# Layer 1 of one 384-token block: each 384-column matmul issued as a 256-column and a 128-column matmul

## The chip, the cores and the metric

The kernel runs on one core of a Trainium2 chip. The metric is device time in microseconds (us) for one execution, the median of the runs of one kernel. A profile is one further execution with the hardware profiler on; it has its own time.

## The reference, cut to what matters

The reference is a random-feature attention followed by a two-layer network with an ELU between the layers:

```python
q_p, k_p = phi(q_s), phi(k_s)          # exp(x @ omega.T - |x|^2/2 - max) / sqrt(128)
kv = einsum('bhsm,bhsd->bhmd', k_p, v);  z = sum(k_p, axis=2)
attn = einsum('bhsm,bhmd->bhsd', q_p, kv) / (einsum('bhsm,bhm->bhs', q_p, z)[..., None] + 1e-6)
x = attn.transpose(0, 2, 1, 3).reshape(4608, 512)
h = x @ w_in                           # layer 1: 512 -> 2048
g = where(h > 0, h, exp(min(h, 0)) - 1)
out = g @ w_out                        # layer 2: 2048 -> 512
```

There are 8 batches of 8 heads, 576 tokens each, so 4608 tokens of 512 features; the network's inner width is 2048.

## The kernel before, in words

The network is computed in a form that keeps nearly full fp32 precision at the matmul rate of the shorter type fp32r: every operand is split into a high part and a low remainder, and a product is the sum of three matmuls, high by high, high by low and low by high.

The 4608 tokens are taken in eight blocks of 384 (blocks 0 to 7; "the eighth block" is number 7) and then in three wide blocks of 512 tokens, which use a scheme with seven products instead of eight (functions `wide1` and `wide2`). Blocks 0 to 2 go through the 16 slices of 128 inner features in two halves, blocks 3 to 7 in one go. A step is one block and one slice f:

- `layer1` (from L1007): for each of four chunks c of 128 input features, three matmuls add into one PSUM tile `ph` of 128 inner features by 384 tokens: weights `wh` by tokens `xh` (L1021), `wh` by `xl` (L1022), `wl` by `xh` (L1023). The weights (128 by 128) are the stationary operand, the tokens the moving one. That is 12 matmuls of 384 columns a step. Each matmul carries its own weight load: the profile has one LDWEIGHTS for each MATMUL, also where two in a row have the same stationary operand.
- the ELU on that tile: ScalarE (L1030, L1031), then VectorE (L1034), then the split into two tiles `g` (L408, L1042).
- `layer2` (from L1046): for three groups of 128 tokens, three products in two halves of 256 columns each, added into the banks `acc` (L1057). That is 18 matmuls of 256 columns a step.

While block 7 runs, VectorE, ScalarE and the DMA queues also prepare the weights of the wide blocks (tiles `rw` and `tw`); the attention is over by then.

The order on each engine is made by a planner in the program: every piece of work is entered with an engine, an estimated cost and a due time (class `Plan`), and the planner writes out one fixed order for each engine. The cost that it is given for three matmuls of layer 1 is `mm(n, 3)` on L1027, and the change does not touch it. At run time the engines keep that order and wait for each other by semaphores.

The code around the change:

Of the kernel before, what the change touches and what calls it, by code (L numbers as in the profile page):

```python
# [25 lines left out]
NC = DM // P  # L26
# [115 lines left out]
class Plan:  # L142
# [19 lines left out]
    def op(self, eng, ns, due, fn, reads=(), writes=(), nbytes=0, alt=None, port=False, tiled=False):  # L162
        n = len(self.tasks)
        engs = {eng: (ns, 0.0)}
        for e, *t in alt or ():
            engs[e] = tuple(t)
        for e in engs:
            if e not in ("PE", "SP"):
                engs[e] = (engs[e][0] * SLACK, engs[e][1])
        f = fn if alt is not None else lambda e: fn()  # L170
        deps, bufs = set(), set()
        for k in reads:
            if k in self.writer:
                deps.add(self.writer[k])
            self.readers.setdefault(k, []).append(n)
        for k in writes:
            if k in self.writer:
                deps.add(self.writer[k])
            deps.update(self.readers.pop(k, ()))
            self.writer[k] = n  # L180
        for k in (*reads, *writes):
            b = k[0] if isinstance(k, tuple) else k
            if isinstance(b, Buf):
                bufs.add(b)
        deps.discard(n)
        for b in bufs:
            b.left += 1
        for b in bufs:
            if b.left == 1:
                b.need = sum(c.key == b.key and c.left == 1 for c in bufs)  # L190
        locks = [e for e in engs if e == "POOL" or e == "DVE" and port]
        self.tasks.append((engs, due, f, deps, bufs, nbytes, locks, tiled))
# [134 lines left out]
def other(kind, *engs):  # L327
    return () if ALT[kind] is None else [(eng, ns, ALT[kind]) for eng, ns in zip(engs[::2], engs[1::2])]


def mm(n, m=1):

    return m * ((227.2 if n == 512 else 0.467 * n) - (0 if n == 512 else 4 if n == 384 else 6.2))


def act(n, psum=False, ptr=False):
    return (55 if psum else 101) + 0.833 * n + (93 if ptr else 0)


def dve(n, fast=False):  # L340
    return 69 + n / (1.92 if fast else 0.96)
# [7 lines left out]
def performer_elu_kernel(  # L349
# [14 lines left out]
    nc = tc.nc  # L364
# [33 lines left out]
    xh = const.tile([P, NC, RING], F32R, name="xh")  # L398
    xl = const.tile([P, NC, RING], F32R, name="xl")
# [4 lines left out]
    def copy(e, dst, src):  # L404
        if e == "ACT":
            nc.scalar.copy(dst, src)  # L406
        else:
            nc.vector.tensor_copy(dst, src)  # L408
# [588 lines left out]
    def ring(blk):  # L997

        o = (blk * TB) % RING
        keys = []  # L1000
        for b in range(2):
            for half, (s0, n) in enumerate(((0, 256), (256, S - 256))):
                if o < b * S + s0 + n and b * S + s0 < o + TB:
                    keys += [(b, hp, half, e) for hp in range(NHP) for e in range(4)]
        return keys

    def layer1(F, due):  # L1007
        blk, f = STEPS[F][:2]
        o = (SLOT[blk] if blk > 2 else blk) * TB
        w = w1c.pop(F)  # L1010
        p = Buf(ps, [P, 512], F32, "ph", f"ph_{F}", 2)
        e = Buf(sb, [P, TB], F32, "e", f"e_{F}", 2)
        n = BLOCKS[blk]
        g = gt[F] = [Buf(sb, [P, 512], F32R, "g", f"g_{F}_{z}", 6) for z in range(2)]

        def ph():
            return p()[:, 0:n]

        def mms(c):
            wh, wl = w()[:, 0, c * P:(c + 1) * P], w()[:, 1, c * P:(c + 1) * P]  # L1020
            nc.tensor.matmul(ph(), wh, xh[:, c, o:o + n], start=(c == 0), stop=False)  # L1021
            nc.tensor.matmul(ph(), wh, xl[:, c, o:o + n], start=False, stop=False)  # L1022
            nc.tensor.matmul(ph(), wl, xh[:, c, o:o + n], start=False, stop=(c == NC - 1))  # L1023

        for c in range(NC):
            reads = [("x3h", SLOT[blk], c), ("x3l", SLOT[blk], c)] if blk > 2 else [(z, k) for k in ring(blk) if k[1] == c for z in ("xh", "xl")]
            op("PE", mm(n, 3), due + 0.5 * c, lambda c=c: mms(c), [*reads, (w, "h"), (w, "l")], (p, ("f", blk, f)) if c == 0 else (p, ("fl", blk, f)) if c == 3 else (p,))  # L1027
        due += 2

        op("ACT", act(n, True), due, lambda: nc.scalar.activation(e()[:, 0:n], ph(), AF.Relu, scale=-1.0), (p,), (e,))  # L1030
        op("ACT", act(n), due + 0.2, lambda: nc.scalar.activation(e()[:, 0:n], e()[:, 0:n], AF.Exp, scale=-1.0), (e,), (e,))  # L1031
        op(
            "DVE", dve(n), due + 0.8,
            lambda: nc.vector.scalar_tensor_tensor(ph(), e()[:, 0:n], -1.0, ph(), ALU.add, ALU.max), (p, e), (p,),  # L1034
        )
        first, second = ("ACT", act(n, True)), ("DVE", dve(n))
        if blk:
            first, second = second, first
        op(*first, due + 1.2, lambda x: copy(x, g[0]()[:, 0:n], ph()), (p,), (g[0],), alt=other("g_hi", *second))
        op(  # L1040
            "DVE", dve(n), due + 1.5,
            lambda: nc.vector.tensor_tensor(g[1]()[:, 0:n], ph(), g[0]()[:, 0:n].bitcast(F32), ALU.subtract),  # L1042
            (p, g[0]), (g[1],),
        )
# [606 lines left out]
    for n in range(len(SEGMENTS)):  # L1651
        blk, f0, f1 = SEGMENTS[n]
# [14 lines left out]
    for s in range(NSB):  # L1667
        n = NS0 + s
# [88 lines left out]
```

## Time and profile before

| | us |
|---|---|
| median of 2 runs | 999.24 |
| the runs | 998.59 and 999.88 |
| profiled execution | 997.4 |
| its span, first to last instruction | 995.6 |
| TensorE busy in the span | 980.9 (99%) |
| VectorE busy | 868.0 (87%) |
| ScalarE busy | 719.1 (72%) |

A matmul's busy time in the profile overlaps that of the next one, since matmuls are pipelined; so the cost of a matmul in a stream is read from the distance between the starts of two that follow each other, not from its own length. The same holds for weight loads. PE is the matmul side of TensorE, PEld its weight loads.

### The profile page before, as it was taken

The numbers are of one execution on the slowest core, as the hardware profiler recorded it, in microseconds if no ns is written. First come the engines' busy times: TensorE is split into PE (matmuls) and PEld (weight loads), VectorE is DVE, ScalarE is ACT, GpSimd is POOL, SyncE is SP. The second block draws the span as 40 slices with busy tenths as digits, with TensorE's granted clock in tenths as the row PEclk, the third lists the DMA queues.
The fourth block names the chain that finished last, engine by engine and source line by source line (L and its number), as shares of the span: only waits on it lengthen the run. The fifth ranks groups of instructions, "written<-read, shape, count | busy, mean of one in ns | idle before, by whom it ended". The sixth has DMA issues, their size and how long they took to land.

```text
span 995.6 us, 27205 instructions
## 1 busy us (share of the span) xinstructions
PE 980.9 (99%) x9282; PEld 942.8 (95%) x9282; DVE 868.0 (87%) x3205; ACT 719.1 (72%) x1985; POOL 517.0 (52%) x695
## 2 busy tenths in 40 slices
PE   9999999999999999999999999999999999999997
PEld 8788899999999999999999999999999999999997
DVE  6998887888789999998999998899999979878866
ACT  7877876787667877887788787745546777777774
POOL 2465666687467787887787876710002232222321
PEclk9999999999999999999999999999999999999999
DMA  7455777777776867676676767388978776766762
GB/s 240 143 195 165 251 258 270 246 246 234 246 232 218 260 198 240 214 246 206 227 234 217 232 218 234 118 282 284 333 257 311 264 233 207 235 219 201 231 189 64
DMA packets 94249, 226.40 MB, mean 227 GB/s; under 512 B 23072, under 2 KB 34976, under 8 KB 94112
## 3 DMA queue, kind: packets, MB, share of 16 engines
q1 hardware_dynamic: 94112, 224.67, 69.2%
q8 instruction: 74, 1.21, 0.5%
q14 instruction: 63, 0.52, 0.2%
HBM read 187.40 MB, written 37.22 MB: 226 GB/s over the span
## 4 chain that ended last, share of the span: by engine, by line
PE 81%; DVE 11%; ACT 3%; issue 2%; DMA 1%; POOL 1%; SPq 1%; DVEq 0%; POOLq 0%
PE acc L1057 22%; PE ph L1021 8%; PE acs L1567 8%; PE ph L1023 8%; PE ph L1022 8%; PE A L1409 5%; PE B L1409 4%; PE pn L878 3%; PE pkv L654 3%; PE ppq L586 3%; PE ppk L586 2%; PE ppq L520 1%; PE pkv L714 1%; DVE rw L411 1%; PE ppk L520 1%
## 5 line engine op out<-in xcount | busy, mean ns | idle before, releaser
L1057 PE MATMUL acc<-w2h,g 128*128 128x256 f32 x1536 | 273.8, 278 | 0.0
L1057 PEld LDWEIGHTS acc<-w2h,g 128*128 128x128 f32 x1536 | 225.6, 188 | 3.6 <-issue 3.5
L1021 PE MATMUL ph<-xh,w1c 128*128 128x384 f32 x512 | 175.7, 343 | 1.5 <-DVE g L1042 1.5
L1023 PE MATMUL ph<-xh,w1c 128*128 128x384 f32 x512 | 172.6, 337 | 0.0
L1022 PE MATMUL ph<-xl,w1c 128*128 128x384 f32 x512 | 172.4, 337 | 0.0
L411 POOL TENSOR_TENSOR gq<-yh,gq 128x256 fp32r<-128x256 f32 x48 | 41.9, 873 | 241.7 <-ACT gq L406 224.8
L1057 PE MATMUL acc<-w2l,g 128*128 128x256 f32 x768 | 150.6, 277 | 0.0
L1057 PEld LDWEIGHTS acc<-w2l,g 128*128 128x128 f32 x768 | 116.3, 188 | 0.0
L1030 ACT ACTIVATE e<-ph 128x384 f32<-128x384 f32 x128 | 62.5, 489 | 63.9 <-PE ph L1023 63.1
L1021 PEld LDWEIGHTS ph<-xh,w1c 128*128 128x128 f32 x512 | 96.1, 188 | 8.0 <-issue 3.7
L1023 PEld LDWEIGHTS ph<-xh,w1c 128*128 128x128 f32 x512 | 96.2, 188 | 0.0
L1022 PEld LDWEIGHTS ph<-xl,w1c 128*128 128x128 f32 x512 | 96.2, 188 | 0.0
L411 POOL TENSOR_TENSOR hq<-hq,den 128x512 f32<-128x512 f32 (+1 forms) x96 | 81.0, 849 | 27.2 <-DVE den L785 22.6
L411 POOL TENSOR_TENSOR tk<-xk,tk 64x576 fp32r<-64x576 f32 x48 | 68.8, 1433 | 45.3 <-ACT tk L406 20.2
L1034 DVE SCALAR_TENSOR_TENSOR ph<-e,ph 128x384 f32<-128x384 f32 x128 | 71.2, 556 | 15.7 <-ACT e L1031 14.9
L776 DVE CUSTOM_DVE_ANT_0 junk<-hq,pz 128x128 f32<-128x128 f32 (+1 forms) x320 | 74.3, 280 | 6.7 <-PE pz L754 5.3
L496 ACT ACTIVATE hk<-hk,nbk 128x128 f32<-128x128 f32 x216 | 68.5, 392 | 13.8 <-POOL nbk L612 13.3
L411 POOL TENSOR_TENSOR tq<-xq,tq 64x576 fp32r<-64x576 f32 x48 | 68.6, 1428 | 15.9 <-DVE tq L408 11.4
L1042 DVE TENSOR_TENSOR g<-ph,g 128x384 fp32r<-128x384 f32 x128 | 70.3, 550 | 7.0 <-ACT g L406 4.6
L496 ACT ACTIVATE hq<-hq,nbq 128x128 f32<-128x128 f32 x216 | 68.4, 396 | 3.8 <-POOL nbq L612 3.6
L1031 ACT ACTIVATE e<-e 128x384 f32<-128x384 f32 x128 | 67.5, 528 | 1.8
L968 POOL TENSOR_TENSOR u_w<-u_w,raw_w 128x512 int32<-128x512 int32 x32 | 43.1, 1350 | 45.2 <-DVE u_w L965 18.0
(208 smaller groups left out, 2644.5 us busy)
## 6 DMA issues: line engine op xcount, KB each, us to landing
w1c<-w1s SPq DMA_DIRECT2D x112, 512.0 KB, 4.3
wp<-w1t SPq DMA_DIRECT2D x48, 512.0 KB, 4.0
raw_w<-in_w_dram SPq DMA_DIRECT2D x32, 512.0 KB, 4.5
xk<-in_kx_dram SPq DMA_DIRECT2D x24, 576.0 KB, 5.6
xq<-in_qx_dram SPq DMA_DIRECT2D x24, 576.0 KB, 4.3
wp<-w1s SPq DMA_DIRECT2D x24, 512.0 KB, 4.7
v<-in_v_dram SPq DMA_DIRECT2D x32, 325.0 KB, 4.0
w1s<-w1c SPq DMA_DIRECT2D x16, 512.0 KB, 3.8
```

Of the source, the lines that this page charges most:

```text
L411: (nc.vector if e == "DVE" else nc.gpsimd).tensor_tensor(*args)
L496: nc.scalar.activation(h()[:, j, :], src(j), AF.Exp, bias=nb()[:, j:j + 1], scale=-1.0)
L776: nc.vector.tensor_tensor_reduce(out=junk()[r], in0=h()[r, j, :], in1=pz()[r, a * P:(a + 1) * P], scale=1.0, scalar=EPS, op0=ALU.mult, op1 ...
L1021: nc.tensor.matmul(ph(), wh, xh[:, c, o:o + n], start=(c == 0), stop=False)
L1022: nc.tensor.matmul(ph(), wh, xl[:, c, o:o + n], start=False, stop=False)
L1023: nc.tensor.matmul(ph(), wl, xh[:, c, o:o + n], start=False, stop=(c == NC - 1))
L1031: op("ACT", act(n), due + 0.2, lambda: nc.scalar.activation(e()[:, 0:n], e()[:, 0:n], AF.Exp, scale=-1.0), (e,), (e,))
L1034: lambda: nc.vector.scalar_tensor_tensor(ph(), e()[:, 0:n], -1.0, ph(), ALU.add, ALU.max), (p, e), (p,),
L1042: lambda: nc.vector.tensor_tensor(g[1]()[:, 0:n], ph(), g[0]()[:, 0:n].bitcast(F32), ALU.subtract),
L1057: nc.tensor.matmul(a()[:, c], x()[:, ts], w[:, f, c], start=(f == f0 and n == 0 and not c.start), stop=(f == f1 - 1 and n == 2 and c.start ...
L1409: nc.tensor.matmul(o, at(a, i), u[b][:, i], start=(start and fresh_bank and i == 0 and n == 0), stop=(i == 1 and n == 2), skip_group_check ...
L1567: nc.tensor.matmul(bank()[:, z * TH:(z + 1) * TH], g()[:, a * TH + z * P:a * TH + z * P + P], w(b), start=(j == 0 and z == 0 and m == 0), ...
```

## The change

In block 7 alone, each of the three products of a chunk is issued as two matmuls with the same stationary operand: one over the first 256 tokens of the block and one over the last 128. Both halves lie in the one PSUM bank of `ph`. The flag that begins an accumulation stands on the first matmul of the tile, the flag that ends it on the last. The other seven blocks go through the same new loop with a single piece of 384.

```diff
         def mms(c):
             wh, wl = w()[:, 0, c * P:(c + 1) * P], w()[:, 1, c * P:(c + 1) * P]
-            nc.tensor.matmul(ph(), wh, xh[:, c, o:o + n], start=(c == 0), stop=False)
-            nc.tensor.matmul(ph(), wh, xl[:, c, o:o + n], start=False, stop=False)
-            nc.tensor.matmul(ph(), wl, xh[:, c, o:o + n], start=False, stop=(c == NC - 1))
+            cut = ((0, 256), (256, n)) if blk == 7 else ((0, n),)
+            for k, (a, x) in enumerate(((wh, xh), (wh, xl), (wl, xh))):
+                for s0, s1 in cut:
+                    nc.tensor.matmul(
+                        p()[:, s0:s1], a, x[:, c, o + s0:o + s1],
+                        start=(c == 0 and k == 0 and s0 == 0), stop=(c == NC - 1 and k == 2 and s1 == n),
+                    )
```

The order on TensorE where block 7 begins, before (`ph` is the layer 1 tile, `acc` a layer 2 bank, `w1c` the layer 1 weights):

```order
L1057 MATMUL acc_0_1_10861<-w2h,g_1_11965 128x256 x2
L1021 MATMUL ph_12041<-xh,w1c_11930 128x384
L1022 MATMUL ph_12041<-xl,w1c_11930 128x384
L1023 MATMUL ph_12041<-xh,w1c_11930 128x384
L1057 MATMUL acc_0_2_10885<-w2h,g_0_11955 128x256 x2
```

and in the changed kernel, at the same place:

```order
L1061 MATMUL acc_0_1_10861<-w2h,g_1_11965 128x256 x2
L1024 MATMUL ph_12041<-xh,w1c_11930 128x256
L1024 MATMUL ph_12041<-xh,w1c_11930 128x128
L1024 MATMUL ph_12041<-xl,w1c_11930 128x256
L1024 MATMUL ph_12041<-xl,w1c_11930 128x128
L1024 MATMUL ph_12041<-xh,w1c_11930 128x256
L1024 MATMUL ph_12041<-xh,w1c_11930 128x128
L1061 MATMUL acc_0_2_10885<-w2h,g_0_11955 128x256 x2
```

Three matmuls have become six, and nothing else has moved: the work of layer 2 stands before and after them as it did. This repeats 64 times (16 steps of four chunks).

On VectorE the same instructions stand in the same order; only what they wait for differs. For the first step of block 7, before:

```order
L1034 SCALAR_TENSOR_TENSOR ph_12041<-e_12079,ph_12041 128x384 [waits Activation_49]
L411 TENSOR_TENSOR tw_12067<-tw_12067 128x256 [waits DVE_49]
L408 CAST g_0_12107<-ph_12041 128x384 [waits DVE_49,PE_49]
L411 TENSOR_TENSOR tw_12067<-tw_12067 128x256 [waits DVE_49]
L1042 TENSOR_TENSOR g_1_12116<-ph_12041,g_0_12107 128x384 [waits DVE_49,PE_49]
```

and in the changed kernel:

```order
L1038 SCALAR_TENSOR_TENSOR ph_12041<-e_12091,ph_12041 128x384 [waits PE_49,Activation_49]
L411 TENSOR_TENSOR tw_12079<-tw_12079 128x256 [waits DVE_49]
L408 CAST g_0_12125<-ph_12041 128x384 [waits DVE_49]
L411 TENSOR_TENSOR tw_12079<-tw_12079 128x256 [waits DVE_49]
L1046 TENSOR_TENSOR g_1_12137<-ph_12041,g_0_12125 128x384 [waits DVE_49]
```

The first instruction of the three that belong to layer 1 now names TensorE as well as ScalarE: it waits for the matmuls of its own tile, for which ScalarE, which it waits for anyway, has waited already.

## Rows read from the trace of the kernel before

**Rows 1.** Profile page: busy time of engines, granted clock, the chain's shares.

```profile
PE 980.9 (99%) x9282; PEld 942.8 (95%) x9282; DVE 868.0 (87%) x3205; ACT 719.1 (72%) x1985; POOL 517.0 (52%) x695
...
PEclk9999999999999999999999999999999999999999
...
PE 81%; DVE 11%; ACT 3%; issue 2%; DMA 1%; POOL 1%; SPq 1%; DVEq 0%; POOLq 0%
```

**Rows 2.** Stretches: block 7's layer 1, then the wide blocks in two parts.

```profile
core 0: us, PE busy (x) PEld busy (x) DVE busy (x) ACT busy (x) POOL busy (x), PEclk, DMA share, GB/s
682.22:746.04 63.82, 63.82 (x458) 63.82 (x457) 60.56 (x139) 31.05 (x65) 0.00 (x0) 1.00 0.88 300
746.04:830.00 83.96, 81.52 (x695) 79.94 (x695) 75.47 (x191) 62.13 (x173) 20.74 (x23) 1.00 0.76 258
830.00:995.60 165.60, 159.25 (x1390) 158.49 (x1388) 132.34 (x336) 117.38 (x324) 40.47 (x50) 0.99 0.61 193
```

**Rows 3.** L1021, 682 to 746 us: count, ns min/median/max, first and last start.

```profile
L1021 PEld LDWEIGHTS ph<-xh,w1c x64: 187/188/188, 682.1 to 745.3; 128*128 128x128 f32 x64
L1021 PE MATMUL ph<-xh,w1c x64: 332/334/336, 682.2 to 745.5; 128*128 128x384 f32 x64
```

**Rows 4.** Order of time inside block 7: start us, length us, engine, line.

```profile
692.84 0.33 PE L1021 MATMUL ph<-xh,w1c 128*128 128x384 f32 x1
692.84 0.19 PEld L1022 LDWEIGHTS ph<-xl,w1c 128*128 128x128 f32 x1
693.01 0.34 PE L1022 MATMUL ph<-xl,w1c 128*128 128x384 f32 x1
693.01 0.19 PEld L1023 LDWEIGHTS ph<-xh,w1c 128*128 128x128 f32 x1
...
693.18 0.34 PE L1023 MATMUL ph<-xh,w1c 128*128 128x384 f32 x1
693.19 0.19 PEld L1021 LDWEIGHTS ph<-xh,w1c 128*128 128x128 f32 x1
...
693.36 0.34 PE L1021 MATMUL ph<-xh,w1c 128*128 128x384 f32 x1
```

**Rows 5.** Chain, 746 to 790 us: twelve 256-column matmuls of the wide blocks.

```profile
788.69 1.36 PE acs L1567 x12
```

**Rows 6.** Lengths as in rows 3: L1409 from 746, L1021 from 50, L800.

```profile
L1409 PE MATMUL A<-xh,wp x96: 276/276/388, 748.1 to 823.9; 128*128 128x256 f32 x96
...
L1021 PE MATMUL ph<-xh,w1c x58: 332/336/448, 58.1 to 149.9; 128*128 128x384 f32 x58
...
L800 PEld LDWEIGHTS pt<-ident,hq x72: 137/140/197, 26.2 to 120.6; 128*128 128x128 f32 x72
L800 PE MATMUL pt<-ident,hq x72: 270/273/329, 26.3 to 120.7; 128*128 128x128 f32 x72
```

**Rows 7.** Order of time: PE at 768.8 us, where it had waited.

```profile
768.85 0.97 PE L1409 MATMUL A<-xh,wp 128*128 128x256 f32 x6 [0.25 <-DVE A L1364]
...
768.85 0.77 PEld L1409 LDWEIGHTS A<-xh,wp 128*128 128x128 f32 x6 [0.45 <-DVE A L1364]
```

**Rows 8.** Order of time in the attention: short matmuls, each with its load.

```profile
12.74 1.87 PEld L714 LDWEIGHTS pkv<-v,hk 128*128 128x128 f32 x16
12.85 1.90 PE L714 MATMUL pkv<-v,hk 128*128 128x65 f32 x16
...
26.23 0.90 PEld L800 LDWEIGHTS pt<-ident,hq 128*128 128x128 f32 x8
```

**Rows 9.** Waits of PE from 746 us on: total, times, longest.

```profile
PE A L1409 <- ACT c L406: 1.1, 1, 1.1
PE B L1409 <- DVE c L1433: 0.6, 1, 0.6
PE B L1409 <- DVE B L1364: 0.4, 2, 0.3
PE A L1409 <- DVE A L1364: 0.3, 1, 0.3
```

**Rows 10.** Order of time: end of block 7's last ELU on ScalarE and VectorE.

```profile
746.95 0.52 ACT L1031 ACTIVATE e<-e 128x384 f32<-128x384 f32 x1
...
747.92 0.56 DVE L1034 SCALAR_TENSOR_TENSOR ph<-e,ph 128x384 f32<-128x384 f32 x1
```

## The prediction

> **What bounds the kernel now.** I read the profile's page first: TensorE (PE) is busy for 99% of the span, its granted clock is at the higher of its two levels (2.4 GHz) in every slice, and the chain of work that ended last lies on PE for 81% [rows 1]. Then the stretches: block 7's layer 1 runs from 682.22 to 746.04 us, and PE is busy for 63.82 of these 63.82 us, with VectorE close behind at 60.56 [rows 2]. So inside the block nothing keeps PE waiting, and time that its instructions gain or lose there moves everything behind it, unless a later wait takes it up. After the block PE is idle for a little: 83.96 less 81.52 us up to 830 us [rows 2].
>
> A busy PE is not yet PE at its best, because matmuls overlap in the record. So the third view is the order of time, where I read only the starts. Three 384-column matmuls in a row start at 692.84, 693.01 and 693.18, and the next one at 693.36: 0.52 us for three, 0.173 each [rows 4]. For 256 columns the wide blocks give twelve in 1.36 us, 0.113 each [rows 5].
>
> The same view shows how weight loads hide. Each load starts at the same hundredth as the matmul in front of its own: 692.84 and 692.84, 693.01 and 693.01 [rows 4]. It runs one matmul ahead, never two. A load therefore has just one matmul's time in which to stay hidden, and the question is how long it really takes; its recorded 0.188 us [rows 3] is longer than a whole 256-column slot, so it overlaps the next load's and can't be the answer.
>
> Three rows give the answer. First, where PE had to wait and a matmul starts together with its own load, both at 768.85 [rows 7], the matmul is recorded with up to 388 ns where the usual one of its line has 276: 112 more. For layer 1 the same difference is 448 less 336, again 112 [rows 6]. That is a load with nothing to hide behind. Second, in the attention sixteen matmuls of only 65 columns, each with its own load, keep their loads (1.87 - 0.19) / 15 = 0.112 us apart [rows 8], though by the columns they should be quick. Third, the only matmuls with 128 moving columns that stand in an unbroken row, the transposes of L800, have loads (0.90 - 0.14) / 7 = 0.109 apart [rows 8]. A load of 128 weight columns in this type costs about 0.112 us. A 256-column matmul (0.113) just covers it, a 384-column one covers it easily, and a 128-column one cannot.
>
> **The change part by part.** It removes 64 x 3 = 192 matmuls of 384 columns (64 on each of three lines; [rows 3] has those of one) and puts in 192 of 256 and 192 of 128 columns, with 192 more loads. Nothing else is moved on PE.
>
> - Taken out: 64 runs of three at 0.52 us, 33.3 us.
> - The 256-column pieces: 192 x 0.113 = 21.7 us. During each of them the load for the 128-column piece runs, hidden.
> - The 128-column pieces: by columns they take 0.173 - 0.113 = 0.060 us (or half of 0.113, 0.057). In this time the load for the next 256-column matmul has to run, and it needs 0.112. The slot becomes 0.112, of which 0.052 is PE standing with the load uncovered. 192 x 0.112 = 21.5 us.
> - Sum: 21.7 + 21.5 - 33.3 = **+9.9 us** on PE. Every fourth triple ends a step and the next matmul is one of layer 2; its load is of the same kind and has the same 0.112 to run.
>
> The 128-column matmul in this type with its own load occurs nowhere before, so its slot has to be bounded. Below: if the load hid completely, 0.057, which makes the pair 0.170 instead of 0.173 and the change worth -0.6 us. Above: if the whole load stood bare ahead of each such piece, 0.057 + 0.112 = 0.169 [rows 6], +20.9 us. I take 0.112, because the rows nearest in shape (short moving side, a load each) lie at 0.109 and 0.112.
>
> The Trainium skill, "TensorE: Matmul & The Clock Gate", section "Back-to-back issue gap", speaks for the lower end: at full clock it puts the distance between matmuls at N / 2.4 + 2.5 ns, for which I estimate 56 for 128 columns, 109 for 256 and 162.5 for 384, so that the sum would be +0.5 us. The 65-column matmuls speak against its use here, since they go by their loads. The same section gives about 81 ns for 128 columns in a stream of loads and matmuls, by which the sum would be some +4 us.
>
> What else changes costs nothing. The wait for PE that the first VectorE instruction of each ELU now names is for matmuls that ScalarE has waited for before it. 192 more matmuls are 2% of 9282 [rows 1] and PE's queue shows no idle time in the block to which they could add.
>
> **What is given back.** A slower PE gives VectorE more time in a stretch where it was 95% busy. PE's idle time from 746 us on is 1.1 + 0.6 + 0.4 + 0.3 = 2.4 us, all of it on ScalarE and VectorE results [rows 9]; each such wait also bares a load. But VectorE can only use the gift as far as it was behind: at the end of the block its ELU instruction starts at 747.92, when its input was done at 746.95 + 0.52 = 747.47 [rows 10], so it lags by 0.45 us. I take 0.5 us given back; the bounds are 0 and 2.4 with some 0.11 for each of the five waits, 3.0.
>
> So the profiled execution goes from 997.4 to 997.4 + 9.9 - 0.5 = 1006.8 us. The median shown is 999.24, 1.8 above the profiled execution, so **1008.6 us** for the median.
>
> **The rivals.**
>
> *By columns (not slower).* If two matmuls in a row with the same stationary operand, or a load that can run further ahead, make the second load free, only columns count: 999.24 - 0.6 = 998.6 us, at best a touch faster than before. It decides as soon as the 128-column slot falls below 0.061 us. For it: nothing in the trace has exactly this shape, and the 65-column rows are of the slower fp32 kind, where one matmul makes two records. Against: layer 2 already issues pairs with the same stationary operand, with a load for each (9282 of both) [rows 1], and the loads in block 7 keep one matmul ahead [rows 4]. The skill's page of the paragraph above is the rule behind it. Chance 0.09; another 0.03 for a load half hidden, a slot near 0.084, 192 x 0.024 = +4.5 us, 1003.7 us.
>
> *All given back that can be.* The load bound holds, but VectorE and ScalarE reach the wide blocks with so much in hand that PE no longer waits for them: 999.24 + 9.9 - 3.0 = 1006.1 us. For it: the waits lie within 85 us of the block. Against: the lag is small, and the work that PE waits for is made from PE's own results. Chance 0.07.
>
> *The load bare at every second piece.* The upper bound: 999.24 + 20.9 = 1020.1 us, if a load did not start before the short matmul was done. Against: the 65-column matmuls, 0.112 with everything in it. Chance 0.03.
>
> **How the numbers follow.** The load-bound case with a small return has 0.78; its own range runs from slots of 0.109 (the transposes; 0.6 us less) to 0.115 (0.6 more), and from 0 to 1.5 us given back: 1007.0 to 1010.2 with some 0.5 for the runs' spread. The range that I give, 1004.5 to 1011, takes in the second rival as well and leaves out the 0.15 of the others. Two per cent, about what a measurement of this kernel can tell from no change, is 20 us: only the last rival passes it. Faster by over 2% has no case (0.01), slower by over 2% has 0.04, and 0.95 lies within.
>
> **What would show it.** Right: in block 7, starts of a 256- and a 128-column matmul 0.113 and about 0.112 us apart, loads too at that distance; the block some 10 us longer than 63.8, PE busy in all of it; VectorE's share in it down to about 82%; PE's waits after it at most as before. Wrong: 128-column starts followed within 0.06 us by the next, with a block of about 63 us; or a block ten us longer and an end that moved far less, which would make the waits the larger story; or a granted clock below its higher level inside the block, which no stretch here before 830 us shows [rows 2].

## The result and the profile after

The changed kernel takes 1010.57 us (median of 2 runs, 1009.92 to 1011.21) against 999.24 us, a ratio of 1.0113 with a 95% interval of 1.007 to 1.0157: some 11 us slower, where 9.4 were forecast. Five runs of it beside nine of before, below, give 1.0102 (1.0084 to 1.012). Its profiled execution takes 1011.21 us with a span of 1009.4.

The page answers to [rows 1]: 192 more matmuls and 192 more loads, the busy shares and the granted clock nearly as they were.

```profile
PE 993.1 (98%) x9474; PEld 954.2 (95%) x9474; DVE 869.2 (86%) x3205; ACT 719.3 (71%) x1985; POOL 515.7 (51%) x695
...
PEclk9999999999999999999999999999999999999999
...
PE 81%; DVE 10%; ACT 3%; issue 2%; DMA 2%; SPq 1%; POOL 0%; DVEq 0%; POOLq 0%
```

Cut into the same stretches as [rows 2], each moved to where block 7 and the wide blocks begin now (columns as there):

```profile
683.86:758.30 74.44, 74.44 (x650) 74.44 (x649) 62.48 (x141) 31.60 (x65) 0.00 (x0) 1.00 0.76 258
758.30:842.26 83.96, 80.88 (x683) 78.72 (x683) 73.66 (x184) 60.48 (x168) 19.16 (x22) 1.00 0.75 255
842.26:1009.40 167.14, 160.79 (x1403) 160.04 (x1402) 133.25 (x340) 118.84 (x328) 40.85 (x50) 0.99 0.60 193
```

Block 7 is 74.44 us long instead of 63.82, so 10.62 us of the difference lie in it, with PE busy throughout, VectorE's share down from 95% to 84% and the clock at its higher level. It begins 1.6 us later than before, which lies within the spread: two profiles of the kernel before (the second is below) begin it 4 us apart. And the stretch from its end to the last instruction is 251.1 us instead of 249.5, of which more below.

Inside the block the weight loads are the rows to read. This is the PEld side, in order of time (start, length, engine, line; neighbours of one line are merged, with their count):

```profile
701.93 0.30 PEld L1024 LDWEIGHTS ph<-xl,w1c 128*128 128x128 f32 x2
702.16 0.54 PEld L1024 LDWEIGHTS ph<-xh,w1c 128*128 128x128 f32 x4
702.63 0.30 PEld L1024 LDWEIGHTS ph<-xl,w1c 128*128 128x128 f32 x2
702.86 0.30 PEld L1024 LDWEIGHTS ph<-xh,w1c 128*128 128x128 f32 x2
703.09 0.30 PEld L1061 LDWEIGHTS acc<-w2h,g 128*128 128x128 f32 x2
```

Two loads, one pair of pieces, every 0.23 us: 702.63 to 702.86 to 703.09, and four from 702.16 to 702.63. Ten loads take 703.09 - 701.93 = 1.16 us, 0.116 each. Over the whole block, by the starts of the single loads, a short matmul's slot is 0.108 us on average and a long one's 0.122, 0.230 for the pair. A product now costs 0.23 us where a 384-column matmul took 0.173 [rows 4]. The forecast had 0.113 + 0.112 = 0.225.

The matmuls' own starts need care here. On this record a 256-column matmul starts about 0.06 us after the short one in front of it, and a short one some 0.17 us after the long one, as if the short matmul had been quick. I read this as a recorded start that lies ahead of the moment at which the weights are in: such a 256-column matmul is also recorded as longer, 0.334 us instead of 0.276 (rows below). Over a pair the two distances add to 0.23. The loads' starts show without this shift what paces the stream.

### The profile page after: what moved, and what is told of

Same layout as the page of the kernel before. It is cut to its first block, busy times and chain, and to the rows that moved or that the text cites. A ratio compares the mean times of both kernels' runs of the same rounds, so it can differ in the third digit from the quotient of the medians.

```text
span 1009.4 us, 27599 instructions
## 1 busy us (share of the span) xinstructions
PE 993.1 (98%) x9474; PEld 954.2 (95%) x9474; DVE 869.2 (86%) x3205; ACT 719.3 (71%) x1985; POOL 515.7 (51%) x695
## 4 chain that ended last, share of the span: by engine, by line
PE 81%; DVE 10%; ACT 3%; issue 2%; DMA 2%; SPq 1%; POOL 0%; DVEq 0%; POOLq 0%
PE ph L1024 24%; PE acc L1061 22%; PE acs L1571 8%; PE A L1413 5%; PE B L1413 4%; PE pn L878 3%; PE pkv L654 3%; PE ppq L586 3%; PE ppk L586 2%; PE ppq L520 1%; DMA xq<-in_qx_dram 1%; PE ppk L520 1%; PE pkv L714 1%; DVE rw L411 1%; DVE junk L776 1%
## 5 line engine op out<-in xcount | busy, mean ns | idle before, releaser
L1024 PE MATMUL ph<-xh,w1c 128*128 128x384 f32 (+2 forms) x1152 | 307.9, 325 | 1.5 <-DVE g L1046 1.5
L1024 PEld LDWEIGHTS ph<-xh,w1c 128*128 128x128 f32 x1152 | 201.5, 188 | 8.0 <-issue 3.7
L1024 PE MATMUL ph<-xl,w1c 128*128 128x384 f32 (+1 forms) x576 | 176.2, 324 | 0.0
L1024 PEld LDWEIGHTS ph<-xl,w1c 128*128 128x128 f32 x576 | 103.3, 188 | 0.0
L411 POOL TENSOR_TENSOR tq<-xq,tq 64x576 fp32r<-64x576 f32 x48 | 68.5, 1428 | 15.5 <-DVE tq L408 10.5
L408 DVE CAST g<-ph 128x384 fp32r<-128x384 f32 x112 | 61.4, 548 | 5.7 <-PE acc L1061 4.3
L600 DVE CUSTOM_DVE_ANT_0 hk<-ppk,p2k 128x128 f32<-128x128 f32 x216 | 52.5, 285 | 9.8 <-ACT p2k L406 8.4
```

What stands on the lines that cost most here:

```text
L411: (nc.vector if e == "DVE" else nc.gpsimd).tensor_tensor(*args)
L1024: nc.tensor.matmul(p()[:, s0:s1], a, x[:, c, o + s0:o + s1], start=(c == 0 and k == 0 and s0 == 0), stop=(c == NC - 1 and k == 2 and s1 == n),
```

## The experiments

Each kernel below is the changed one with one more edit, if nothing else is said. Times are medians, ratios against the kernel before on the same chip.

**The changed kernel again.**

> The changed kernel again, for the size of the difference. Load theory (a weight load costs some 0.11 us and can hide behind one matmul only): +9.4 us forecast on the median, +10.6 us by the length of block 7 in its first profile, so a ratio near 1.010. Rival, part of the first difference is spread of the executions outside the block: the block's length comes out at 74 us again, and what lies before and behind it changes by a us or two without order.

1009.48 us (5 runs) against 999.52 (9 runs): +10.0 us, ratio 1.0102 (1.0084 to 1.012). Its block 7:

```profile
684.43:758.87 74.44, 74.44 (x650) 74.44 (x649) 62.38 (x141) 31.60 (x65) 0.00 (x0) 1.00 0.76 257
```

To the hundredth the length of the first profile. So the block is the measure to compare kernels by: the timed difference has an interval of some 2 us to either side, the block's length none that can be seen.

**The cut at 192.**

```diff
-            cut = ((0, 256), (256, n)) if blk == 7 else ((0, n),)
+            cut = ((0, 192), (192, n)) if blk == 7 else ((0, n),)
```

> Block 7's layer 1 matmuls cut at 192 instead of 256: 192 + 192 columns. Load theory: 192 columns need about 0.087 us, less than a load, so both slots are load-bound, 0.108 to 0.112 each, a pair 0.216 to 0.224: +8.2 to +9.7 us against before. Columns theory (only columns count): no change. Fixed price for every extra matmul: as the 256 + 128 cut, +10.6 us.

1008.45 us, ratio 1.009 (1.0074 to 1.0105), +8.9 us. The block (the first row), and its loads in order of time:

```profile
681.22:755.09 73.87, 73.87 (x650) 73.87 (x649) 62.32 (x141) 31.57 (x65) 0.00 (x0) 1.00 0.77 260
```

```profile
700.86 0.31 PEld L1024 LDWEIGHTS ph<-xh,w1c 128*128 128x128 f32 x2
...
702.21 0.30 PEld L1061 LDWEIGHTS acc<-w2h,g 128*128 128x128 f32 x2
```

Twelve loads in 702.21 - 700.86 = 1.35 us, 0.1125 each, for 192 columns that would need some 0.087 us by the columns. Columns theory falls. The block is 10.05 us longer than before; a fixed price for every extra matmul would fit this run too.

**The cut at 320.**

```diff
-            cut = ((0, 256), (256, n)) if blk == 7 else ((0, n),)
+            cut = ((0, 320), (320, n)) if blk == 7 else ((0, n),)
```

> Cut at 320: 320 + 64 columns. Load theory: the 320-column slot is some 0.143 us by its columns, the 64-column slot still a whole load, 0.108 to 0.112, a pair 0.251 to 0.255: +15 to +16 us, dearer than the 256 + 128 cut with the same columns and the same number of matmuls. Fixed price for every extra matmul: +10.6 us, as that cut. Columns theory: no change.

1015.5 us, ratio 1.0155 (1.014 to 1.0171), +16.0 us. The block is 79.64 us long, 15.82 more than before:

```profile
685.57:765.21 79.64, 79.64 (x650) 79.64 (x649) 62.64 (x141) 31.45 (x65) 0.00 (x0) 1.00 0.71 241
```

The same columns and the same number of matmuls as in the change, and 5.2 us more in the block. A fixed price for every matmul falls here: the short slot doesn't get cheaper with its columns (0.108 us on average, as in the change), while the long one gets dearer (0.149). By the load, 64 columns leave more of it uncovered than 128.

**Three pieces of 128.**

```diff
-            cut = ((0, 256), (256, n)) if blk == 7 else ((0, n),)
+            cut = ((0, 128), (128, 256), (256, n)) if blk == 7 else ((0, n),)
```

> Three pieces of 128 columns: 384 extra matmuls and loads. Load theory: three slots of 0.108 to 0.112, 0.324 to 0.336 in place of 0.173: +29 to +31 us. Fixed price for every extra matmul, by the 256 + 128 cut: twice its cost, +21 us. Columns theory: no change.

1030.78 us, ratio 1.0312 (1.0295 to 1.0329), +31.3 us. Nine loads of short pieces, from 701.35 to 702.35:

```profile
701.35 0.75 PEld L1024 LDWEIGHTS ph<-xh,w1c 128*128 128x128 f32 x6
702.01 0.42 PEld L1024 LDWEIGHTS ph<-xl,w1c 128*128 128x128 f32 x3
702.35 0.75 PEld L1024 LDWEIGHTS ph<-xh,w1c 128*128 128x128 f32 x6
```

1.00 / 9 = 0.111 us for each 128-column matmul in an unbroken stream of them: the price of which the kernel before had no row, and nearly twice its 0.057 by the columns.

**256 + 256: columns for nothing.** The second piece is widened to 256 columns by taking the last 128 tokens twice; the second copy goes to bank columns that nothing reads.

```diff
+                    dst, src = p()[:, s0:s1], x[:, c, o + s0:o + s1]
+                    if s0:
+                        dst = p()[:, s0:512].rearrange("p (r x) -> p r x", r=2)
+                        src = src.unsqueeze(1).to_broadcast([P, 2, P])
```

> The 256 + 128 cut of block 7, but the second matmul has 256 columns: the last 128 tokens twice, the second time into 128 columns of the PSUM bank that nobody reads. 192 x 128 columns of added work. Load theory: a 256-column slot costs what a load costs, about 0.113, so a pair is 0.226 to 0.228: +10.1 to +10.5 us against before, the same as the 256 + 128 cut or less. Fixed price for every extra matmul, or columns theory: 192 x 0.056 = 10.7 us more than the 256 + 128 cut, +21 us against before.

1008.59 us, ratio 1.0079 (1.0057 to 1.0101), +8.1 us, and the block and its loads:

```profile
682.64:756.08 73.44, 73.44 (x651) 73.44 (x649) 62.20 (x141) 31.49 (x65) 0.00 (x0) 1.00 0.78 261
```

```profile
700.21 0.30 PEld L1028 LDWEIGHTS ph<-xh,w1c 128*128 128x128 f32 x2
...
701.57 0.30 PEld L1065 LDWEIGHTS acc<-w2h,g 128*128 128x128 f32 x2
```

This block does a third more columns in layer 1 than the changed kernel's and is 1.00 us shorter. Twelve loads take 701.57 - 700.21 = 1.36 us, 0.113 each. So 128 columns were free: the slot is as long without them. The block comes out lower than was expected, 9.6 us above before instead of 10.1 to 10.5. The layer 1 slots are the expected 0.113 each; what had not been thought of is layer 2, whose 264 slots in the block came down from 0.1154 us on average to 0.1133.

The timed kernels so far leave one rival that had not been written down: a least distance of some 0.11 us between any two matmuls, whatever sets it, would give all these times too. The traces speak against it. In the changed kernel PE waits before the matmul at 821.57 us, whose load starts together with it:

```profile
821.57 0.75 PEld L1413 LDWEIGHTS A<-xh,wp 128*128 128x128 f32 x6 [0.64 <-DVE A L1368]
821.57 0.95 PE L1413 MATMUL A<-xh,wp 128*128 128x256 f32 x6 [0.44 <-DVE A L1368]
822.36 0.84 PE L1571 MATMUL acs<-w_qh,gq 128*128 128x256 f32 x6
```

These six matmuls take 822.36 - 821.57 = 0.79 us, where six 256-column slots take 0.68. PE had just been idle, so a least distance had nothing to delay, and yet 0.11 us more are spent: the length of one load.

The recorded lengths say the same, though the profile models the ends of matmuls. The lines are from block 7 of the changed kernel (first two), the cut at 320 (next two), the cut at 192 (fifth) and the three pieces (last); the last number but one is the mean length in ns:

```profile
L1024 PE MATMUL ph<-xl,w1c 128*128 128x256 f32 x64 | 21.4, 334 | 0.0
L1024 PE MATMUL ph<-xl,w1c 128*128 128x128 f32 x64 | 14.3, 223 | 0.0
L1024 PE MATMUL ph<-xl,w1c 128*128 128x320 f32 x64 | 25.0, 391 | 0.0
L1024 PE MATMUL ph<-xl,w1c 128*128 128x64 f32 x64 | 12.3, 192 | 0.0
L1024 PE MATMUL ph<-xl,w1c 128*128 128x192 f32 x128 | 24.9, 276 | 0.0
L1024 PE MATMUL ph<-xl,w1c 128*128 128x128 f32 x192 | 31.9, 275 | 0.0
```

A 256-column matmul has 276 ns behind one of its kind, 334 behind one of 128 columns, and up to 388 with the whole load bare [rows 6]: 0, 58 and 112 more. A 128-column one has 223 behind a long one and 275 behind one of its kind, 52 more; a 320-column one 304 behind 256 columns and 391 behind 64, 87 more; a 192-column one 252 behind 256 columns and 276 behind one of its kind, 24 more. With 64, 128, 192 and 256 columns in front the wait falls from 87 to 0, as the part of a load does that they leave uncovered.

**The pieces grouped by length.** Within a chunk, three matmuls of 256 columns, then three of 128:

```diff
-            for k, (a, x) in enumerate(((wh, xh), (wh, xl), (wl, xh))):
-                for s0, s1 in cut:
+            for s0, s1 in cut:
+                for k, (a, x) in enumerate(((wh, xh), (wh, xl), (wl, xh))):
```

> The same 192 + 192 matmuls of 256 and 128 columns, in another order: within a chunk first the three of 256, then the three of 128. Load theory: still one load a matmul; the two 256-column matmuls that follow one of their kind go back to 0.113, the short ones are 0.108 to 0.112 as in the cut into three: a triple 3 x 0.113 + 3 x 0.110 = 0.669 or a little over, +9.5 us, about 1 us less than the alternating order (whose 256-column loads were 0.120 to 0.128 apart). Rival, the price belongs to the change of bank columns between pieces and not to the loads: a third of the changes are left (two of six against six of six), so +3 to +4 us.

1010.06 us, ratio 1.0093 (1.0077 to 1.011), +9.5 us; the block 74.26 us:

```profile
683.07:757.33 74.26, 74.26 (x650) 74.26 (x649) 62.37 (x141) 31.48 (x65) 0.00 (x0) 1.00 0.77 258
```

The rival that laid the price on changes of bank columns falls. But the block came down by 0.18 us and not by the 1 us that was expected. Over the 192 pairs, the few thousandths by which a mixed pair (0.229, 0.173 + 10.62 / 192) exceeds 0.113 + 0.111 are 0.9 us. The starts of the single loads show where they went: layer 1 did come down, from 44.18 to 43.50 us, but the 264 slots of layer 2 in the block went up from 30.31 to 30.82. So the alternation does cost something in layer 1, and the grouping moves most of it behind layer 1's short matmuls. What sets these thousandths stays open: only where all matmuls have 256 columns (256 + 256) is every slot in the block 0.113 to 0.114.

**The cut in block 5.**

```diff
-            cut = ((0, 256), (256, n)) if blk == 7 else ((0, n),)
+            cut = ((0, 256), (256, n)) if blk == 5 else ((0, n),)
```

> The 256 + 128 cut in block 5 instead of block 7, while the attention still runs beside it. Load theory with TensorE as the bound there too: the same 192 pairs, +10 us. Rival, TensorE has slack among the attention's waits in block 5 and takes the loads up: clearly less, +3 to +7 us.

1007.9 us, ratio 1.0079 (1.0063 to 1.0094), +7.4 us by the medians. Block 5 before, and then with the cut:

```profile
507.88:599.48 91.60, 91.59 (x985) 87.91 (x986) 86.19 (x425) 73.41 (x220) 72.73 (x112) 1.00 0.70 227
```

```profile
507.60:609.30 101.70, 101.66 (x1178) 98.41 (x1179) 87.15 (x427) 74.08 (x220) 73.59 (x112) 1.00 0.63 205
```

Block 5 is 10.1 us longer; in the ten other profiles, none of which cuts it, it is 91.1 to 92.5. TensorE is the bound there as well, attention or not, and the rival with slack falls by the block's length. The interval of the timed difference (6.3 to 9.4 us) lies a little below that, but the profile shows nothing given back behind the block: block 6 takes 82.7 us as before, block 7 63.82, and the rest 249.8. What the 2 to 3 us are stays open.

**Before, profiled once more.**

> The kernel before once more, for a second profile: block 7 again 63.8 us long; the time from its end to the last instruction shows whether the 1.2 to 2.2 us by which this stretch was longer in the profiles of the cut kernels is an effect of the cut (again 249.5 us here) or spread (250 to 252 us).

One run of 1002.33 us, with a span of 1000.5. Block 7 is again 63.82 us long:

```profile
686.31:750.13 63.82, 63.82 (x459) 63.82 (x458) 60.35 (x139) 30.94 (x65) 0.00 (x0) 1.00 0.87 300
```

It begins at 686.31 instead of 682.22, so one and the same kernel differs by 4 us ahead of the block. From the block's end to the last instruction it takes 1000.5 - 750.1 = 250.4 us. With the first profile, the block 5 kernel and the one below, four profiles without a cut in block 7 have 249.5 to 250.4 there, mean 249.9; seven with one have 250.3 to 251.7, mean 251.1. The two sets overlap, but in the profiles the cut kernels come out about 1 us longer behind the block, and none gets anything back. The timed runs don't show this 1 us: in the seven experiments with a cut block the timed difference lies from 2.7 us below to 0.4 above what that block gained in length, 0.9 below on average. So the time by the clock is less certain, by a us or two, than the length of the block.

**Longer matmuls instead of shorter ones.** The kernel before, with each pair of 256-column matmuls of layer 2 made into one of 512, in all eight blocks:

```diff
-                    for c in (slice(0, TH), slice(TH, DM)):
+                    for c in (slice(0, DM),):
```

> The kernel before with the opposite edit in layer 2 of all eight blocks: each pair of 256-column matmuls with the same stationary operand becomes one of 512 columns, 1152 in place of 2304, with half the loads. Load theory: a 256-column matmul just covers a load, so little is to be had: from 0 (two slots of 0.113 become 0.227) to -4 us (the slots of block 7's layer 2 were 0.1155 on average; if all of the 0.002 is the load's, 2304 x 0.002 = 4.6 us). Fixed price for every extra matmul of some 0.05 us: 1152 fewer would give some -60 us. Rival on the other side: long matmuls pay 0.451 ns a column, as the 384-column ones do, 0.231 a slot: 0 to +5 us.

1001.92 us (11 runs) against 1000.17 (15), ratio 1.0024 (1.0014 to 1.0035): slower by 1.8 us by the medians. In order of time on PE, three 512-column matmuls start at 702.00, 702.23 and 702.46, and the next matmul at 702.69:

```profile
702.00 0.39 PE L1057 MATMUL acc<-w2h,g 128*128 128x512 f32 x1
702.23 0.39 PE L1057 MATMUL acc<-w2l,g 128*128 128x512 f32 x1
702.46 0.39 PE L1057 MATMUL acc<-w2h,g 128*128 128x512 f32 x1
702.69 0.33 PE L1021 MATMUL ph<-xh,w1c 128*128 128x384 f32 x1
```

0.23 us each, 0.45 ns a column as with the 384-column ones; two 256-column ones had taken 0.227 [rows 5]. 1152 matmuls fewer gained nothing, so no fixed price shows for a matmul whose load is covered.

No kernel here beats the one before.

## Why the prediction was right, and where it was off

*The load costs 0.112 us and hides behind one matmul only.* Right, and shown in four ways: 0.111 and 0.1125 us a slot where every piece is short, a dearer pair when the short piece gets shorter (cut at 320), no dearer one when it gets columns for which the load's time is enough (256 + 256), and 0.11 us more where a load stands bare behind an idle PE. The rows of before that carried this were the pair of lengths with and without a covered load [rows 6, 7] and the loads of the 65-column matmuls [rows 8].

One row of the same group seemed to say otherwise and was passed over: the transposes of L800 have 329 ns at most and 273 as a rule [rows 6], which by the same subtraction makes a load of 56. The changed kernel explains it. A 128-column matmul with its load covered is recorded with 223 ns, so the usual 273 of a stream of them holds half a load already, and 329 - 223 = 106 is near the 109 that the forecast took from their loads.

Two readings of the prediction were wrong and cost it nothing: 32 of the 64 triples, not every fourth, have layer 2 behind them (the slot there is 0.108 us either way); and L520 and L654 have 128 moving columns in a row as well, though with a stationary operand of half the size.

*The sum on PE, +9.9 us.* Right in kind, 0.7 us too small: 10.62 by the block. The term that was mis-sized is the pair, put at 0.113 + 0.112 and measured at 0.230, and in it the long piece: 0.122 and 0.108. The sum had taken the 256-column slot from streams of that shape alone.

*The block stays bound by PE and the cost lies on the path.* Right: PE is busy for 74.44 of 74.44 us.

*0.5 us given back by VectorE.* Not borne out by the profiles, and with it the rival that gave back 3 us. The forecast took PE's waits behind the block for a backlog of VectorE's. The first three of them show that they are not. They come 19.1, 22.9 and 47.9 us after the block in the changed kernel, within 0.1 us of their places before. This is the largest, before and after, 19.07 and 19.14 us behind the block, and then the list of the changed kernel:

```profile
765.11 0.98 PE L1409 MATMUL A<-xl,wq 128*128 128x256 f32 x6 [1.10 <-ACT c L406]
777.44 0.98 PE L1413 MATMUL A<-xl,wq 128*128 128x256 f32 x6 [1.10 <-ACT c L406]
```


```profile
PE A L1413 <- ACT c L406: 1.1, 1, 1.1
PE A L1413 <- DVE A L1368: 0.7, 2, 0.4
PE B L1413 <- DVE B L1368: 0.7, 2, 0.5
PE B L1413 <- DVE c L1437: 0.5, 1, 0.5
```

That is nearly the list of [rows 9], which the 10 us that VectorE was given had no part in shortening. What sets them was not tried. What changed is a later place. The chain of waits of the kernel before leads there through the load of the next wide block's tokens (start, length, what):

```profile
800.00 6.36 DMA xw<-xd
806.38 0.62 ACT xl L406
```

and that of the changed kernel through the same load, 0.93 us longer:

```profile
812.19 7.29 DMA xw<-xd
819.51 0.62 ACT xl L406
```

Behind it PE waits for 0.44 us, at 821.57 us (the row above), at a place where it had not waited before. Both loads are issued some 54 us after the block's end (800.00 - 746.04 and 812.19 - 758.30). Why it lands later is not settled: in the four profiles without a cut in block 7 it has landed 59.7 to 60.7 us after the block, in the seven with one 60.7 to 61.7. Over the eleven profiles a later landing goes with a longer stretch from the block to the end (60.0 us with 249.8, 61.7 with 251.7), so the load is the likely source of the 1 us; no experiment tried it alone.

*The number.* The two misses, a pair 0.7 us too cheap and a return that did not come, point the same way and did not cancel. The first median, 1010.57 us, lies above the 1007.0 to 1010.2 that the prediction gave its main case, whose lower end also left out the 0.5 for the spread; the second, 1009.48, lies within. That the first fell within the wider range owes something to the margin.

*The rivals.* Columns alone: against the measured 0.111 us for 128 columns. The load bare at every second piece, +20.9 us: no, the block has half of that. The estimate of some +4 us from the figure of 81 ns in the Trainium skill, "TensorE: Matmul & The Clock Gate", section "Back-to-back issue gap", and that of +0.5 us from its N / 2.4 + 2.5, do not hold for these fp32r matmuls, each with its own load, where the slot is 111 ns. The section "LDWEIGHTS (loading the stationary operand)" of that page has columns / 1.2 ns; for 128 columns I estimate 107, and the 111 of the trace agrees within 4%.

## What to carry to other kernels

In this kernel each matmul brings its weight load, and the load could hide only behind the matmul in front of it. So the least useful moving size is the one whose columns take as long as a load, 256 here; below it a piece cost a load, whatever its columns (64, 128 or 192), and above it nothing was gained by going longer (512). To price a shape that a trace does not hold, look for the same load where it stands bare: the difference between the longest and the usual length of one line's matmuls gave 0.112 us before anything was run. This needs a line whose usual matmul has its load covered; the transposes of L800, where it has not, gave half.

## What had not been expected of the hardware

- Columns can be free: 192 times 128 more columns in the short pieces made the block 1.00 us shorter (73.44 against 74.44).
- Per column, the 384- and 512-column fp32r matmuls were no cheaper than the 256-column ones: 0.451, 0.45 and 0.443 ns (0.173, 0.23 and 0.1133 us).
- The recorded start of a matmul that waits for its weights seems to lie some 0.06 us ahead of its work (256 columns behind 128: started 0.06 us after it, recorded 0.058 us longer); the distance between loads shows the pace.
- Matmuls of mixed lengths are a little slower than their parts: the layer 2 slots of the block, 256 columns each, took 0.1154 us on average beside 384-column matmuls, and 0.1133 where layer 1 had 256 columns as well.
